# Attention and capped experts on one core: own first turn, quartered score tile, reordered closing steps

## The chip, the cores and the metric

The kernel runs on one core of a Trainium2 chip. TensorE (PE) multiplies, VectorE (DVE), ScalarE (ACT) and GpSimd (POOL) work on SBUF and PSUM, and SyncE (SP) and GpSimd issue most of the transfers. The metric is the device time of one execution in microseconds (us).

## The reference

Block-causal attention over 8 batches and 8 heads (576 positions, head size 64, blocks of 64), then a layer of 8 experts (512 to 1024 and back), each of which takes at most `capacity` (80) of the 4608 tokens.

```python
scores = where(block_i >= block_j, q @ k.T / sqrt(64), -1e9)
x      = softmax(scores) @ v                      # (4608, 512)
logits = x @ w_gate;  expert = argmax(logits);  gate = softmax(logits)[expert]
for e in range(8):                                # the 80 tokens with the largest gate
    out[tok] = gate[tok] * (relu(x[tok] @ w1[e]) @ w2[e])   # all other rows are 0
```

## The kernel before

**Attention** runs in turns, one for each pair of heads (32 pairs, 4 to a batch). `Pair.load` brings q and k in 32-column pieces (8 transfers of 72 KB on SP's queue, five turns ahead); `prep` transposes a piece-wise tile on VectorE, and for q GpSimd scales it into `QT`, a tile with a block of zeros in it (two passes, L476). `scores` multiplies for the five query tiles: "78", "56", "34", "12" of 128 rows, and the small tile "08", which holds the first and the last block of 64 rows. Before, the small tile is made of two products of full 128-row width per head that add up, each half of whose weight is the block of zeros (L495), and then a mask product (L506) writes large negative numbers over a block of the 56 tile. `max` takes row maxima on VectorE, `merge` the joint maximum of the first and last blocks' rows, `soft` the exponentials on ScalarE, which also sum the rows. `back` transposes the probabilities on TensorE block by block (L554) in groups B, A, C, L; `take` copies them out of PSUM on ScalarE or VectorE (L585); `values` multiplies with v (L574); `flip` turns the result on VectorE (L328), and `store` sends a batch to DRAM (`xs`) on SP's queue.

The order of each engine's work in this part is written out by hand: the list `TURN` (L38) is walked once per turn, and each entry names a pair relative to the turn's index and a step, so that a turn holds the scores and exponentials of the next pair and the transposes and values of its own. The turns before index 0 walk the same list with the pairs that exist; turn -1 thus runs the scores, maxima and exponentials of pair 0 in `TURN`'s order, with all the exponentials after `merge`. `LAST` is the list of the last turn. An engine takes its instructions in that order and waits at each for what it needs.

**Gating** is a side work of small steps: when a batch has been flipped, `enqueue` puts its steps on lists, and entries "pe", "t" and "ta" of `TURN` take one each: `recip`, `logits`, `products`, `shift`, `expo`, `first_of`, `weight`, `turn`, `turn2`, `placed`. They end in the table `Wt`. The last batch's steps are written out behind the loop (L685 to L715): row sums, the copies of the last values, logits, both last flips, `store`, `logits_out` (one half by ScalarE, one by VectorE), and so on to `placed`.

**Constants** are made in turn -2 (`constants`, `constants2`) ahead of the transposes of pair 0. The output rows are cleared by 18 transfers of 512 KB of zeros in the last five turns, on GpSimd's queue (L665).

**Selection** (L751 to L853): each partition's best values, ranks by products with triangular matrices, counts by compare-and-sum on VectorE and ScalarE, one-hot matrices, and products that pick token numbers into `gi`. From here on the order within an engine is the scheduler's, but for `issue_after`, which puts one instruction behind another. `warm` issues products whose result nobody reads: WARM[0] at the start, and WARM[1] to WARM[4] behind `turn2` of the last batch but one, `turn2` of the last, the ranks and the picks.

**Experts**: GpSimd gathers 80 rows for each expert (`xg`, L849), VectorE divides them by the row sums (`divide`, L937), TensorE transposes them (L963), multiplies with w1 (L954) and w2 (L1004), and GpSimd scatters the results (L1013). Weights come in 2 MB loads on SP's queue; three are there early, the fourth is issued behind the last batch's last store (L738), two more when the first gather has landed, the others after the fourth gather or as buffers come free.

## Time and profile before

| | us |
|---|---|
| runs | 420.0, 422.56, 422.8 (median 422.56) |
| profiled execution | 421.09 |
| its span | 419.3 |
| TensorE busy in it | 384.6 (92%) |
| ScalarE busy | 300.4 (72%) |
| VectorE busy | 279.6 (67%) |
| GpSimd busy | 141.7 (34%) |

Busy times are sums over the whole span. The turns run from about 16 to 286 us, gating and selection to about 315, the experts to the end. The end of a matmul is modelled, so TensorE's busy time holds waits as well. A line such as L554 is the line of the code that issued the instruction.

### The profile page before, as it was taken

What the parts mean: (1) busy time and instruction counts of PE and PEld (TensorE: products, weight loads), DVE (VectorE), ACT (ScalarE), POOL (GpSimd) and SP (SyncE); (2) the same over time, 40 slices, a digit from 0 to 9 for tenths busy, and PEclk for the clock granted to TensorE, in tenths of its full rate; (3) what the DMA queues carried; (4) which work ended last, traced back from release to release, by engine and by line L of the source; (5) the groups of instructions that cost most, each with busy time, mean ns of one, the idle gap of its engine ahead of it and who ended that gap; (6) DMA issues with size and microseconds to landing.
All of it is one profiled execution on the core that took longest, in us unless ns stands there. A gap on an engine that the chain in (4) does not pass through costs nothing. (4 is left out here: it accounts for less than half of the span.)

```text
span 419.3 us, 13895 instructions
## 1 busy us (share of the span) xinstructions
PE 384.6 (92%) x5359; PEld 256.4 (61%) x5359; DVE 279.6 (67%) x773; ACT 300.4 (72%) x950; POOL 141.7 (34%) x273
## 2 busy tenths in 40 slices
PE   5699999999999999999999999998877899999960
PEld 3566676666766676666676667666557745657420
DVE  5688888998899899899799989988743210100010
ACT  0699999999999999999999999996022132333340
POOL 6035332544336334354434545630246000000010
PEclk9699999999999999999999999999869899999995
DMA  9989999999999979999989899994649999998000
GB/s 122 146 124 181 148 195 142 220 174 144 193 188 173 147 157 169 139 201 173 150 177 155 151 132 327 373 353 114 172 176 292 383 398 388 395 399 316 20 19 19
DMA packets 199287, 84.31 MB, mean 201 GB/s; under 512 B 163677, under 2 KB 182109, under 8 KB 199216
## 3 DMA queue, kind: packets, MB, share of 16 engines
q1 hardware_dynamic: 187728, 56.35, 65.2%
q0 software_dynamic: 9120, 26.72, 21.7%
q8 instruction: 44, 0.72, 0.8%
q10 hardware_dynamic: 2368, 0.30, 0.6%
q14 instruction: 27, 0.22, 0.2%
HBM read 63.21 MB, written 20.33 MB: 199 GB/s over the span
## 5 line engine op out<-in xcount | busy, mean ns | idle before, releaser
L527 ACT ACTIVATE P<-bank,negm 128x192 f32<-128x192 f32 (+2 forms) x320 | 162.2, 591 | 0.0
L499 PE MATMUL bank<-T,qt 64*128 64x320 f32 (+3 forms) x512 | 107.1, 507 | 5.7 <-ACT P L527 3.9
L516 DVE TENSOR_REDUCE negm<-bank 128x1 f32<-128x192 f32 (+1 forms) x192 | 87.8, 472 | 25.9 <-PE bank L506 25.7
L585 ACT COPY PT<-bank 128x512 f32<-128x512 f32 (+1 forms) x190 | 90.3, 586 | 8.0 <-PE bank L554 8.0
L574 PE MATMUL bank<-PT,vn 128*64 128x384 f32 (+5 forms) x768 | 93.8, 384 | 0.9 <-ACT PT L585 0.9
L527 ACT ACTIVATION_READ_ACCUMULATOR P<-bank,negm 128x1 f32 x320 | 89.6, 281 | 0.0
L554 PEld LDWEIGHTS bank<-ident,P 64*128 64x128 f32 x1664 | 65.6, 140 | 19.4 <-ACT PT L585 19.2
L477 POOL TENSOR_SCALAR qt<-T 128x512 f32<-128x512 f32 x64 | 28.0, 449 | 145.8 <-DVE raw L516 131.8
L574 PEld LDWEIGHTS bank<-PT,vn 128*64 128x64 f32 x768 | 47.6, 137 | 40.8 <-issue 31.2
L554 PE MATMUL bank<-ident,P 64*128 64x64 f32 x1664 | 72.2, 226 | 0.0
L499 PEld LDWEIGHTS bank<-T,qt 64*128 64x128 f32 x512 | 43.6, 187 | 20.4 <-issue 7.4
L470 DVE STREAM_TRANSPOSE T<-ld 128x576 f32<-128x576 f32 x64 | 49.1, 768 | 0.2
L516 DVE TENSOR_REDUCE raw<-bank 128x1 f32<-128x64 f32 (+1 forms) x128 | 48.6, 435 | 0.6 <-PE bank L499 0.6
L463 POOL DMA_DIRECT2D vn<-in_v_dram x58 | 45.8, 792 | 1.0 <-PE bank L506 0.7
L954 PE MATMUL ps<-xsT,w 128*64 128x80 f32 x1024 | 40.2, 238 | 2.4 <-issue 1.9
L954 PEld LDWEIGHTS ps<-xsT,w 128*64 128x64 f32 x1024 | 38.0, 141 | 5.9 <-issue 4.6
L1008 DVE SCALAR_TENSOR_TENSOR y<-av,comb,yt 80x512 f32<-80x512 f32 x7 | 5.2, 746 | 50.2 <-ACT yt L1007 50.2
L1004 PE MATMUL av<-w,hT 128*32 128x512 f32 (+1 forms) x280 | 37.5, 594 | 0.0
L1013 POOL DMA_INDIRECT out_dram<-y,si x8 | 7.4, 925 | 78.2 <-DVE y L1008 78.2
L1007 ACT ACTIVATE yt<-ps,gfar 32x512 f32<-32x512 f32 (+1 forms) x18 | 11.4, 635 | 28.5 <-PE ps L1004 28.4
L496 PEld LDWEIGHTS bank<-T,qt 64*128 64x128 f32 x256 | 23.7, 191 | 11.6 <-issue 10.8
L1004 PE MATMUL ps<-w,hT 128*32 128x512 f32 (+1 forms) x72 | 29.1, 547 | 0.0
(175 smaller groups left out, 395.2 us busy)
## 6 DMA issues: line engine op xcount, KB each, us to landing
w<-in_moe_w_dram SPq DMA_DIRECT2D x13, 2048.0 KB, 19.8
ld<-in_q_dram SPq DMA_DIRECT2D x128, 72.0 KB, 4.2
xs<-Y SPq DMA_DIRECT2D x32, 288.0 KB, 5.7
out_dram<-zero POOLq DMA_DIRECT2D x18, 512.0 KB, 7.1
ld<-in_k_dram SPq DMA_DIRECT2D x124, 72.0 KB, 4.2
vn<-in_v_dram POOLq DMA_DIRECT2D x58, 128.0 KB, 4.3
w<-in_moe_w_dram POOLq DMA_DIRECT2D x8, 512.0 KB, 5.9
w<-in_moe_w_dram POOLq DMA_DIRECT2D x8, 256.0 KB, 5.9
```

Of the source, the lines that this page charges most:

```text
L463: eng.dma_start(self.vn[:, h], v[b, h0 + h, 0:512].rearrange("(j p) d -> p j d", p=P))
L470: nc.vector.transpose(t, self.nat[x].rearrange("p g d -> p (g d)"))
L477: nc.gpsimd.tensor_scalar(to, from_, scalar1=SCALE, scalar2=1.0, op0=ALU.mult, op1=ALU.mult)
L496: nc.tensor.matmul(s[h][:, c:c + n], lhsT=q_[:, b0:b0 + P], rhs=k_[:, k0:k0 + n], start=False, stop=False)
L499: nc.tensor.matmul(s[h][:, c:c + n], lhsT=q_[:, BLK + P * t:BLK + P * (t + 1)], rhs=k_[:, 0:n], start=(c == 0), stop=(g == "1"))
L516: nc.vector.tensor_reduce(to[:, b, h:h + 1], self.s[g][h][:, c:c + n], axis=AX.X, op=ALU.max, negate=True)
L527: nc.scalar.activation(Pt[self.i % 2][u][:, h, 0:n], self.s[g][h][:, c:c + n], AF.Exp, bias=self.negm[:, t, h:h + 1], scale=1.0, accum_out ...
L554: nc.tensor.transpose(pt[c][:, n_ * BLK:(n_ + 1) * BLK], row[u][r, h, P * j:P * (j + 1)], ident[r, r])
L574: nc.tensor.matmul(to, lhsT=self.vt[:, h, :] if j == 4 else self.vn[:, h, j, :], rhs=self.PT[:, h, row, b0:b1].rearrange("p b r -> p (b r) ...
L585: (nc.scalar.copy if (eng or TAKE[x]) == "a" else nc.vector.tensor_copy)(*self.out.pop(x))
L954: yield nc.tensor.matmul(dst(b)[64 * c:64 * (c + 1)], lhsT=w_[:, a, col:col + 64], rhs=x_[:, a], start=(a == 0), stop=(a == n - 1))
L1004: last = nc.tensor.matmul(to[col:col + s1 - s0, c0:c1], lhsT=hT[:, a, s0:s1], rhs=w_[:, a, c0:c1], start=(a == ends[0]), stop=(a == ends[1 ...
```

## The change

- The warming products become 8, 5, 5, 2 and 10.
- Turn -1 walks a list of its own, `FIRST`: pair 1's q is prepared ahead of pair 0's scores, each exponential of the 56 tile follows its maximum, the small tile's exponentials come right after `merge`, and so on.
- One exponential of a column of ones (`early_exp`) is issued on ScalarE in turn -4. The constants are made in turn -4, what needs their sums in turn -1, and the rest in turn 1.
- The small tile: one product per head and half, of a 64-column weight, into its own half of the rows, with no block of zeros; `QT` has 576 columns and GpSimd scales them in one pass; the mask of the 56 tile, 64 rows wide, comes ahead of the small tile.
- The clears of the last five turns go to SP's queue.
- Behind the loop: the steps left of the last batch but one come first; the reciprocals come after the values' copies; ScalarE copies both halves of the logits; only the flip of the last pair but one stays ahead of them. The steps of `first_of` and `weight` are interleaved, and the flip of the last pair and the store come after `turn`.
- In the selection the ranks' products keep their written order, the first slot step stands behind the counts, and the one-hot matrices are made in four pieces. `divide` works in four pieces, one per pair of heads, not two.

```diff
-WARM = [8, 10, 5, 2, 12]
+WARM = [8, 5, 5, 2, 10]
...
+FIRST = (
+    (LEAD, "load"),
+    (1, "begin"),
+    (2, "prep", 0),
+    (1, "scores", "2"),
+    (1, "max", "56", 0),
+    (1, "soft", "56", 0),
+    (1, "max", "56", 1),
+    (1, "soft", "56", 1),
+    (1, "scores", "1"),
+    (1, "scores", "3"),
+    (1, "max", "78", 0),
+    (1, "max", "78", 1),
+    (1, "max", "08", 0),
+    (1, "max", "08", 1),
+    (1, "merge"),
+    (2, "prep", 1),
+    (1, "soft", "08", 0),
+    (1, "soft", "08", 1),
+    (1, "soft", "78", 0),
+    (1, "soft", "78", 1),
+    (1, "max", "12", 0),
+    (1, "max", "34", 0),
+    (1, "max", "12", 1),
+    (1, "max", "34", 1),
+    (1, "soft", "12", 0),
+    (1, "soft", "34", 0),
+    (1, "soft", "12", 1),
+    (3, "load_v"),
+)
+
...
-                copy = nc.vector.tensor_copy if c and self.b == B - 1 else nc.scalar.copy
-                copy(lgT[:, BLK + 288 * c:BLK + 288 * (c + 1)], lt[c][:, 0:288])
+                nc.scalar.copy(lgT[:, BLK + 288 * c:BLK + 288 * (c + 1)], lt[c][:, 0:288])
...
                 self.T[1] = t
                 return
             self.T[0] = q_ = QT[self.i % 2]
-            ends, t_ends = [x_.rearrange("p (b c) -> p b c", c=BLK) for x_ in (q_[:, 0:3 * BLK], t)]
-            for to, from_ in ((q_[:, 3 * BLK:], t[:, BLK:]), (ends[:, 0:3:2], t_ends[:, 0:9:8])):
-                nc.gpsimd.tensor_scalar(to, from_, scalar1=SCALE, scalar2=1.0, op0=ALU.mult, op1=ALU.mult)
+            nc.gpsimd.tensor_scalar(q_, t, scalar1=SCALE, scalar2=1.0, op0=ALU.mult, op1=ALU.mult)

         def begin(self):
             self.negm = sm.tile([P, NT, 2], F32, name="negm", bufs=3)
...
         def scores(self, g):

             self.s[g] = s = banks("s" + g)
-            for u, c in GROUPS[g]:
+            rows = [slice(h * D, h * D + D) for h in range(2)]
+            for at, (u, c) in enumerate(GROUPS[g]):
                 t, n = TILES[u]
-                for h in range(2):
-                    r = slice(h * D, h * D + D)
+                last = u == GROUPS[g][-1][0]
+                if g == "2" and last:
+                    self.mask(g, BLK, False)
+                for h, r in enumerate(rows):
                     q_, k_ = self.T[0][r], self.T[1][r]
                     if u == "08":
-                        for b0, k0 in ((0, 0), (BLK, 512)):
-                            nc.tensor.matmul(s[h][:, c:c + n], lhsT=q_[:, b0:b0 + P], rhs=k_[:, k0:k0 + n], start=False,
-                                             stop=False)
+                        for half, b0 in ((0, 0), (BLK, 512)):
+                            nc.tensor.matmul(s[h][half:half + BLK, c:c + n], lhsT=q_[:, b0:b0 + BLK],
+                                             rhs=k_[:, b0:b0 + n], start=False, stop=True)
                     else:
-                        nc.tensor.matmul(s[h][:, c:c + n], lhsT=q_[:, BLK + P * t:BLK + P * (t + 1)], rhs=k_[:, 0:n], start=(c == 0),
-                                         stop=(g == "1"))
-            if g in MASKED:
-                ends = MASKED[g]
-                for h in range(2):
-                    r = slice(h * D, h * D + D)
-                    blocks = s[h].rearrange("p (u c) -> p u c", c=BLK)
-                    nc.tensor.matmul(blocks[:, ends[0]:ends[-1] + 1:max(ends[-1] - ends[0], 1)], lhsT=mrow[r],
-                                     rhs=mneg[r, 0:len(ends)], start=False, stop=True)
+                        nc.tensor.matmul(s[h][:, c:c + n], lhsT=q_[:, P * t - BLK:P * t + BLK], rhs=k_[:, 0:n],
+                                         start=(c == 0), stop=(g == "1"))
+            if g == "3":
+                self.mask(g, P, True)
+
+        def mask(self, g, m, stop):
+
+            ends = MASKED[g]
+            for h in range(2):
+                r = slice(h * D, h * D + D)
+                blocks = self.s[g][h][0:m].rearrange("p (u c) -> p u c", c=BLK)
+                nc.tensor.matmul(blocks[:, ends[0]:ends[-1] + 1:max(ends[-1] - ends[0], 1)], lhsT=mrow[r, 0:m],
+                                 rhs=mneg[r, 0:len(ends)], start=False, stop=stop)

         def group(self, u):
             return [(g, c) for g, us in GROUPS.items() for u_, c in us if u_ == u][0]
...

             for _ in range(4 if i >= n - 5 else 0):
-                clear(cleared)
+                clear(cleared, nc.sync)
                 cleared += 1
-            if i == -2:
+            if i == 1 - LEAD:
+                nc.scalar.activation(early_exp, ramp[:, 2, 0:1], AF.Exp)
                 constants()
+            if i == -1:
                 constants2()
             if i == 1:
                 constants3()
             if i >= 2 and i % 3:
                 next(early, None)
-            for d, what, *args in TURN if i < n - 1 else LAST:
+            for d, what, *args in FIRST if i == -1 else TURN if i < n - 1 else LAST:
                 if what in slots_:
                     slots_[what]()
                 elif 0 <= i + d < n and not (what == "flip" and n - NP <= i + d < n - 2):
...
                 enqueue(batches[(i - flipped) // NP])
         for _ in early:
             pass
+        while not turns:
+            t()
         bt = batches[B - 1]
-        for _ in bt.recip():
-            pass
         to, from_ = pairs[n - 1].out.pop("V0")
         half = to.shape[1] // 2
         pairs[n - 1].take("V1", "v")
         nc.scalar.copy(to[:, 0:half], from_[:, 0:half])
         nc.vector.tensor_copy(to[:, half:], from_[:, half:])
         lt = bt.logits_of()
-        for p_ in pairs[n - 2:]:
-            p_.flip()
-        bt.store()
+        for _ in bt.recip():
+            pass
+        pairs[n - 2].flip()
         bt.logits_out(lt)
-        ta()
-        while not turns:
-            t()
         bt.logits2()
         bt_, mark = turns.pop(0)
         bt_.turn2(banks("av")[0])
...
         bt.expo()
         while small:
             t()
-        for _ in (*bt.first_of(), *bt.weight()):
-            pass
+        found, weighed = bt.first_of(), bt.weight()
+        for g_ in (found, found, found, weighed, found, weighed, weighed):
+            next(g_)
         bt.turn(nc.vector, 2)
+        pairs[n - 1].flip()
+        bt.store()
         bt.turn2(banks("L")[0])
         for _ in bt.placed():
             pass
...
-    vec.scalar_tensor_tensor(slot[:, NH:], cnt_a, 0.5, pen[:, 1], op0=ALU.mult, op1=ALU.add)
+    with tc.issue_after(counted.ins):
+        vec.scalar_tensor_tensor(slot[:, NH:], cnt_a, 0.5, pen[:, 1], op0=ALU.mult, op1=ALU.add)
     vec.tensor_tensor(slot[:, 0:NH], cnt_v, pen[:, 0], op=ALU.add)
-    with tc.issue_after(one_hot(NH, NCAND).ins):
-        one_hot(0, NH)
+    hot = None
+    for c0 in (NH, NH + 3, 0, 3):
+        with ExitStack() as order:
+            if hot is not None:
+                order.enter_context(tc.issue_after(hot.ins))
+            hot = one_hot(c0, c0 + 3)
     for i in (*range(NH, NCAND), *range(NH)):
         picked = nc.tensor.matmul(pick[0:CHUNK, 0:3 * E], lhsT=OH[:, i], rhs=RI[:, i].rearrange("p k e -> p (k e)"),
                                   start=(i == NH), stop=(i == NH - 1))
...

-        v = src[:, 0:DM].rearrange("s (h i r c) -> s h r i c", h=2, i=2, r=NP)
-        r_ = src[:, DM:DM + H].rearrange("s (r h) -> s h r", h=2)
-        d = dst.rearrange("s (r h i c) -> s h r i c", r=NP, h=2, i=2)
-        for h in range(2):
-            last = vec.tensor_tensor(d[:, h], v[:, h], r_[:, h].unsqueeze(2).unsqueeze(3).broadcast_to([CHUNK, NP, 2, 32]),
-                              op=ALU.mult)
+        v = src[:, 0:DM].rearrange("s (h i r c) -> s r h i c", h=2, i=2, r=NP)
+        r_ = src[:, DM:DM + H].rearrange("s (r h) -> s r h", h=2)
+        d = dst.rearrange("s (r h i c) -> s r h i c", r=NP, h=2, i=2)
+        for r in range(NP):
+            last = vec.tensor_tensor(d[:, r], v[:, r], r_[:, r].unsqueeze(2).unsqueeze(3).broadcast_to([CHUNK, 2, 2, 32]),
+                                     op=ALU.mult)
         return last


```

## Rows read from the trace of the kernel before

**Rows 1.** Waits, 27 to 286 us, ScalarE and weight loads: total us, times, longest.

```profile
ACT PT L585 <- PE bank L554: 6.0, 13, 0.6
...
PEld bank L554 <- ACT PT L585: 18.6, 30, 0.6
```

**Rows 2.** Timeline of the opening: start, us, work, count, idle before and its releaser.

```profile
10.32 1.16 DVE L516 TENSOR_REDUCE negm<-bank 128x1 f32<-128x448 f32 x2 [1.68 <-PE bank L506]
...
12.08 1.51 DVE L516 TENSOR_REDUCE raw<-bank 128x1 f32<-128x64 f32 x4
...
12.35 1.28 ACT L527 ACT_TABLE_LOAD   x1 [12.35 <-DVE raw L516]
...
13.63 0.22 DVE L520 SCALAR_TENSOR_TENSOR negm<-raw,lower 128x4 f32<-128x4 f32 x1
13.64 0.63 ACT L527 ACTIVATE P<-bank,negm 128x448 f32<-128x448 f32 x1
...
16.05 2.03 PE L499 MATMUL bank<-T,qt 64*128 64x448 f32 x3 [3.89 <-ACT P L527]
...
20.57 0.58 ACT L585 COPY PT<-bank 128x512 f32<-128x512 f32 x1 [1.83 <-PE bank L554]
...
23.48 0.68 ACT L527 ACTIVATE P<-bank,negm 128x448 f32<-128x448 f32 x1
```

**Rows 3.** Stretches on TensorE: us, busy (count), granted clock, DMA share, GB/s.

```profile
14.00:16.00 2.00, 0.00 (x0) 0.54 1.01 160
...
20.00:21.00 1.00, 1.00 (x24) 0.51 0.86 186
```

**Rows 4.** Timeline of one turn on TensorE, from values to the block transposes.

```profile
155.19 0.28 PE L574 MATMUL bank<-PT,vt 128*64 128x64 f32 x4
...
155.30 0.29 PE L574 MATMUL bank<-PT,vn 128*64 128x64 f32 x4
...
155.52 1.02 PE L499 MATMUL bank<-T,qt 64*128 64x448 f32 x4
...
156.38 0.66 PE L496 MATMUL bank<-T,qt 64*128 64x64 f32 x8
...
156.80 0.25 PE L554 MATMUL bank<-ident,P 64*128 64x64 f32 x1
```

**Rows 5.** Timeline of the end of attention, VectorE.

```profile
293.14 1.43 DVE L328 STREAM_TRANSPOSE Y<-xT 128x576 f32<-128x576 f32 x2
...
294.50 0.42 DVE L353 COPY lgT<-bank 128x288 f32<-128x288 f32 x1
```

**Rows 6.** Timeline from gating to the first divide.

```profile
296.78 4.07 PE L595 MATMUL ps<-identr 128*128 128x512 f32 x10
...
298.99 0.56 DVE L406 TENSOR_TENSOR sp<-Gm,sameE 128x160 f32<-128x160 f32 x2
...
300.77 0.37 PE L415 MATMUL bank<-sp,sameR 128*32 128x40 f32 x16
...
310.24 1.12 POOL L849 DMA_INDIRECT xg<-xs,gi  x1 [4.61 <-DMA w<-in_moe_w_dram]
...
313.38 0.76 DVE L943 TENSOR_TENSOR xn<-xg 80x256 f32<-80x256 f32 x2 [4.04 <-DMA xg<-xs,gi]
```

**Rows 7.** Timeline of SP's queue at the last stores.

```profile
296.76 1.63 SPq L335 DMA_DIRECT2D xs<-Y  x1
298.78 1.27 SPq L288 DMA_DIRECT2D w<-in_moe_w_dram  x1
```

**Rows 8.** DMA issues, one each: KB, us to landing (issued at 312.96, 314.23, 296.76, 298.78).

```profile
xg<-xs,gi POOLq DMA_INDIRECT x1, 4.2
...
xg<-xs,gi POOLq DMA_INDIRECT x1, 8.7
...
xs<-Y SPq DMA_DIRECT2D x1, 288.0 KB, 5.6
...
w<-in_moe_w_dram SPq DMA_DIRECT2D x1, 2048.0 KB, 11.3
```

More of the change, by code (lines that the diff above doesn't have):

```diff
@@ L227, in tile_attn_moe @@
     dl = sm1.tile([P, NT, E + 1], F32, name="dl")
+    early_exp = sm1.tile([P, 1], F32, name="early_exp")
     def constants():
@@ L237, in constants @@
         nc.gpsimd.memset(lgT[:, 0:BLK], 0.0)
-    def constants2():
-        nc.vector.tensor_reduce(sameE, ident.rearrange("p (e j) -> p e j", j=16), axis=AX.X, op=ALU.add)
         nc.gpsimd.memset(sameR3, 0.0)
-        nc.vector.tensor_reduce(sameR, ident.rearrange("p (e j) -> p j e", j=16), axis=AX.X, op=ALU.add)
-        nc.gpsimd.tensor_copy(same.rearrange("p (e j) -> p e j", j=16), sameE.unsqueeze(2).broadcast_to([P, E, 16]))
         nc.gpsimd.memset(ones, 1.0)
@@ L248, in constants2, with constants3 @@
         nc.gpsimd.iota(iota_p, pattern=[[0, 1]], base=0, channel_multiplier=1, allow_small_or_imprecise_dtypes=True)
-        nc.gpsimd.affine_select(out=before, in_=same, compare_op=ALU.is_gt, fill=0.0, base=0,
-                                pattern=[[1, P]], channel_multiplier=-1)
-        nc.gpsimd.affine_select(out=after, in_=same, compare_op=ALU.is_gt, fill=0.0, base=0,
-                                pattern=[[-1, P]], channel_multiplier=1)
-        nc.gpsimd.tensor_tensor(before1, before, ident, op=ALU.add)
-        nc.gpsimd.tensor_tensor(after1, after, ident, op=ALU.add)
         nc.gpsimd.iota(iota_c, pattern=[[1, 16]], base=0, channel_multiplier=0,
                        allow_small_or_imprecise_dtypes=True)
+    def constants2():
+        vec, pool = nc.vector, nc.gpsimd
+        vec.tensor_reduce(sameE, ident.rearrange("p (e j) -> p e j", j=16), axis=AX.X, op=ALU.add)
+        vec.tensor_reduce(sameR, ident.rearrange("p (e j) -> p j e", j=16), axis=AX.X, op=ALU.add)
+        pool.tensor_copy(same.rearrange("p (e j) -> p e j", j=16), sameE.unsqueeze(2).broadcast_to([P, E, 16]))
+        pool.affine_select(out=before, in_=same, compare_op=ALU.is_gt, fill=0.0, base=0,
+                           pattern=[[1, P]], channel_multiplier=-1)
+        pool.affine_select(out=after, in_=same, compare_op=ALU.is_gt, fill=0.0, base=0,
+                           pattern=[[-1, P]], channel_multiplier=1)
+        pool.tensor_tensor(before1, before, ident, op=ALU.add)
+        pool.tensor_tensor(after1, after, ident, op=ALU.add)
+    def constants3():
         nc.vector.tensor_tensor(iota_c16, sameR, iota_c, op=ALU.mult)
         nc.vector.tensor_reduce(iota_r, iota_c16, axis=AX.X, op=ALU.add)
-    def constants3():
         nc.gpsimd.tensor_copy(cf, ci)
@@ L295, in tile_attn_moe @@
     Pt = [{u: pb.tile([P, 2, w], F32, name=f"P{u}_{i}") for u, w in WIDE.items()} for i in range(2)]
-    QT = [pb.tile([P, S + 2 * BLK], F32, name=f"qt{i}") for i in range(2)]
+    QT = [pb.tile([P, S], F32, name=f"qt{i}") for i in range(2)]
     VT = [pb.tile([P, 2, D], F32, name=f"vt{i}") for i in range(4)]
@@ L604, in tile_attn_moe @@
                 nc.gpsimd.memset(ps_[u][:, :, TILES[u][1]:w], 0.0)
-    for t_ in QT:
-        nc.gpsimd.memset(t_[:, BLK:2 * BLK], 0.0)
     for t_ in VT:
@@ L767, in tile_attn_moe @@
     HC = 16 * NH
+    ranked = None
     for h in (1, 0):
         pl = pall[h]
-        for k in range(2):
-            for g in range(2):
-                m = (before, after)[k] if g == h or k == h else (before1, after1)[k]
+        for k, g in ((k, g) for k in range(2) for g in range(2)):
+            m = (before, after)[k] if g == h or k == h else (before1, after1)[k]
+            with ExitStack() as order:
+                if ranked is not None:
+                    order.enter_context(tc.issue_after(ranked.ins))
                 ranked = nc.tensor.matmul(pl[:, g * HC:(g + 1) * HC], lhsT=m,
@@ L828, in one_hot @@
                                  iota_s.unsqueeze(1).broadcast_to([P, c1 - c0, CHUNK]), op=ALU.is_equal)
-    vec.scalar_tensor_tensor(slot[:, NH:], cnt_a, 0.5, pen[:, 1], op0=ALU.mult, op1=ALU.add)
+    with tc.issue_after(counted.ins):
+        vec.scalar_tensor_tensor(slot[:, NH:], cnt_a, 0.5, pen[:, 1], op0=ALU.mult, op1=ALU.add)
     vec.tensor_tensor(slot[:, 0:NH], cnt_v, pen[:, 0], op=ALU.add)
-    with tc.issue_after(one_hot(NH, NCAND).ins):
-        one_hot(0, NH)
+    hot = None
+    for c0 in (NH, NH + 3, 0, 3):
+        with ExitStack() as order:
+            if hot is not None:
+                order.enter_context(tc.issue_after(hot.ins))
+            hot = one_hot(c0, c0 + 3)
     for i in (*range(NH, NCAND), *range(NH)):
```

2 lines of the change are left out of this document (1 added, 1 removed).

## The prediction

> **What bounds the kernel now.** I read the waits by engine over the turns first. From 27 to 286 us ScalarE waited 6.0 us in all, in 13 of the 31 turns, each time for the block transposes of the pair in hand (L554); TensorE's weight loads waited 18.6 us for ScalarE's copies, in 30 turns [rows 1]. So ScalarE's stream sets the pace of the turns, and TensorE touches it only in those 13. What brings that stream forward at its start brings the end forward; what shortens TensorE's turn gains 6.0 us at the most.
>
> Second, the timeline of the opening [rows 2]. The first maxima start at 10.32, after an idle 1.68 of VectorE. The first exponential stands behind the merge and behind a table load of 1.28, and starts at 13.64. TensorE, idle for 3.89, begins pair 1 at 16.05. ScalarE's first copy waits 1.83 more and starts at 20.57, and pair 1's first exponential at 23.48. By the granted clock TensorE ran at 1.2 instead of 2.4 GHz from about 14.1 to 21.0 [rows 3].
>
> Third, one turn on TensorE [rows 4], and last the closing chain from the last logits to the first expert: the two flips, the logits' second copy behind them [rows 5], the spread weights, ten warming matmuls in front of the turning matmuls, the gather, the first divide [rows 6].
>
> **First turn.** Put ahead of the first maximum are one transposition (a flip of the same size is 1.43/2 = 0.71 [rows 5]) and two reductions, which I bound by the 0.58 of a 448-column maximum: 1.87 against a cover of 1.68 [rows 2], and these reductions used to stand ahead of the first transposes, which now start sooner. I take 10.32 as it is; without that cover it would be 1.9 later. The table load moves into the 12.35 that ScalarE idles before it [rows 2]: free. The first exponential then starts at about 10.95, not 13.64. The merge ends at 10.32 + 1.16 + 1.51 + 0.22 = 13.2. Two small exponentials follow (six took 16.05 - 13.64 = 2.41, 0.40 each), so pair 1's scores start at 14.0, **2.05 earlier**. That copy came 4.52 after pair 1's first scores, mostly at half clock: at worst 18.5 now. At full clock it would be 2.3 after, but the five exponentials left end at 17.2 at the latest, so 17.2. The gain at the copy is 2.1 to 3.4. The clock fell in a pause of 3.89 that becomes 1.8, so it may stay, or not: I take **-2.8**. The lower end is -1.0: TensorE spent 16.05 to 21.0 at half clock; if the whole stretch from 14.1 falls on turn 0, 2 us more at half speed give back 1.0. The upper end is -3.4. Past it the loads are ahead, and VectorE is waited for by nobody in [rows 1].
>
> **The quarters, 32 times.** From the small tile's first matmul to the first block transpose it is 156.80 - 156.38 = 0.42 [rows 4], eight matmuls in two row tiles, 0.1 per step. A step of 64 columns with a 64-column weight took 155.30 - 155.19 = 0.11 for two; the same four matmuls followed by another tile shape took 155.52 - 155.30 = 0.22. A change of shape therefore shows as 0.11. The new order has two more (64*128 to 64*64 and back), a mask step (0.06), two steps if all four quarters run at once (0.11), and some 0.05 of weight load no longer hidden: 0.44. If the halves of a head follow each other it is 0.60 with rounding up; if the change of shape is free 0.28. The mark on a turn is -0.14 to +0.18; I take +0.05, as the 0.11 is measured on this engine in this loop. It counts in the 13 turns where ScalarE waits: **+0.65**. Ends: 13 x -0.14 = -1.8, and 31 x 0.18 = +5.6 if the slack of the other turns is used up.
> The Trainium skill (TensorEngine Tiling (Array Packing), Key Properties) says that changing the tiling mode, not just the tile, drains the engine; it gives no time. The 0.11 agrees. Its Theoretical Speedup table says up to 2x for a dimension of 64 or less; by that alone the small tile would save half of its 0.42, about -2.7 over 13 turns, without the drains.
> The single scaling pass over 576 columns in place of two costs nothing: GpSimd is waited for by nobody in [rows 1].
>
> **Clears on SyncE.** 18 issues leave GpSimd's queue and join SP's behind the last loads of q and k; nothing but the stores of batch 6 stands behind them, which no engine needs for two turns. The bytes are the same. Nothing; without that cover the stores would land some microseconds later, still ahead of the gather.
>
> **The closing chain.** The logits' second copy goes from VectorE at 294.50, behind two flips, to ScalarE behind its first copy: 0.4 sooner. The interleaved seven small steps save about 0.2 of waits on one another. Five warming matmuls instead of ten (4.07 for ten [rows 6]) end before the spread weights are ready, so the turning matmuls start at 298.99 + 0.56 and not at 300.77: 1.2 sooner. The last flip, now behind the spread weights, holds the copy into the table for 0.3. Sum at that copy: -0.4 - 0.2 - 1.2 + 0.3 = -1.5. One-hot in quarters and the ranks head by head: -0.2, the gather issued at 308.5 instead of 310.24.
> But the stores of the last batch wait for the last flip. They began when both flips were done, 293.14 + 1.43 = 294.57, and will at 299.55 - 0.6 + 0.71 = 299.7, **5.1 later**. Behind them on SP's queue stands the next weight load: 298.78 [rows 7] goes to 303.9, and its landing 11.3 later [rows 8] to 315.2. The last store, issued at 296.76 and 5.6 in flight, lands at 307.5, just ahead of the gather. So the gather, which had the DMA engines to itself (313.38 - 310.24 = 3.14), now runs beside 2 MB of weights. With loads beside it a fetch took 4.2 (one that met them late) to 8.7 [rows 8]: landing at 311.6 (3.1) to 317.2. I take 4.5, near the row that met them late, since this load is halfway through by then: 313.0, -0.35. The divide in four pieces lets the transposes start on the first: -0.3. Sum **-0.65**; ends: 311.6 - 313.38 - 0.3 = -2.1, and 317.2 - 313.38 - 0.3 = +3.5. Two microseconds more come on top if the missing warming leaves the ranking at half clock; that would fall in the store's shadow.
>
> **Sum.** -2.8 + 0.65 - 0.65 = -2.8. The profiled execution took 421.09 (span 419.3), so 418.3. The runs are 420.0, 422.56 and 422.8, median 1.5 above the profiled one; I forecast **418.5**.
>
> **Rivals.**
> *The gather is not held up.* For it: only one load is in flight, and 3.14 is the clean time. Then the tail gives -2.1 and the sum is -4.25: 416.8. Chance 0.24.
> *The clock takes the opening back.* TensorE still pauses, and the fall at 14.1 came 2 us after its last matmul [rows 3]; all of turn 0 then runs at half clock: -1.0 + 0.65 - 0.65, 420.1. This is also the case in which the reordering hardly does what it says. Chance 0.20.
> *The quarters cost the loop*, the one that ends slower. Place: between the scores of the 448-column tile and the transposes ScalarE's copies wait for. Price: two drains (0.22), the halves in sequence (0.22), the mask (0.06), two weight loads unhidden (0.2): 0.70 against 0.42, +0.28 a turn; 3.6 in the 13 turns, 8.7 if all 31 come to wait. It decides from 0.11 a turn on, where 31 turns eat the 3.45 of the other two terms. At 8.7 the time is 421.09 - 3.45 + 8.7 = 426.3, at 3.6 it is 421.2; I price it at 424. Against it: TensorE waits for ScalarE in 30 turns [rows 1], so it has slack. The drain above is what the skill's rule would charge. Chance 0.13.
> *The forecast*, 417.5 to 420, has 0.38; 0.05 is left for a gather at 8.7 (422).
>
> **How the numbers follow.** About 1% (4.2 us) is what a measurement of this kernel can tell from no change: faster means under 418.3. All of the first rival and a third of the forecast's case lie there: 0.37. Slower (over 426.8) is part of the quarters' case: 0.08. The rest, 0.55, is within 1%. The range goes from 414.2, where the good ends of opening and tail (-3.4 - 2.1) and most of the quarters' (-1.4 of -1.8) meet, to 424.0, which takes in the gather's bad end and the quarters' case up to its price. The likeliest case alone is 417.5 to 420.
>
> **What would show it.** ScalarE's first exponential near 11 and pair 1's first near 20.6; the small tile's matmuls as 64*64 and the distance to the first transpose near 0.44; ScalarE's waits for L554 near 6 us; the turning matmuls close behind the spread weights; stores from 299.7 less the opening's gain, and the first fetch over 4 us from issue to landing. I am wrong if pair 1's first exponential moves by under 1.5, if ScalarE comes to wait for L554 in nearly every turn, or if the first fetch lands in about 3.

## The result, and the profile after

The changed kernel takes **417.4 us** (median of 6 runs, 416.4 to 417.9) against 421.8 for the kernel before beside it: ratio 0.9892, 95% interval 0.9868 to 0.9916, 4.6 us or 1.1% faster. The forecast was 418.5 in a range of 414.2 to 424.0. The time was inside the range, and in part by luck: of the four terms only the opening came as forecast. The quarters' cost did not come, the clears gained where nothing was expected, and the closing chain alone lost time where a gain was forecast, and these misses nearly cancel.

The opening, in the timeline of the changed kernel (start, us, work, count, idle before and its releaser), to be held against [rows 2]:

```profile
2.95 1.28 ACT L703 ACT_TABLE_LOAD   x1 [2.95 <-issue]
...
9.72 1.16 DVE L553 TENSOR_REDUCE negm<-bank 128x1 f32<-128x448 f32 x2
...
10.38 0.63 ACT L564 ACTIVATE P<-bank,negm 128x448 f32<-128x448 f32 x1 [5.94 <-DVE negm L553]
...
12.37 0.22 DVE L557 SCALAR_TENSOR_TENSOR negm<-raw,lower 128x4 f32<-128x4 f32 x1
...
13.47 1.25 PE L532 MATMUL bank<-T,qt 64*128 64x448 f32 x4 [1.82 <-ACT P L564]
...
17.70 0.58 ACT L622 COPY PT<-bank 128x512 f32<-128x512 f32 x1 [0.73 <-PE bank L591]
...
21.06 0.64 ACT L564 ACTIVATE P<-bank,negm 128x448 f32<-128x448 f32 x1
...
24.77 1.02 PE L532 MATMUL bank<-T,qt 64*128 64x448 f32 x4
```

The table load stands at 2.95, the first exponential at 10.38 and not behind the merge, pair 1's scores 2.58 earlier, pair 1's first exponential at 21.06 and not 23.48, the second turn's scores at 24.77 and not 26.90. The clock fell all the same; stretches on TensorE (us, busy (count), granted clock, DMA share, GB/s), against [rows 3]:

```profile
14.00:16.00 2.00, 2.00 (x30) 0.58 0.94 157
...
20.00:21.00 1.00, 1.00 (x9) 0.50 0.89 169
21.00:22.00 1.00, 1.00 (x12) 0.92 0.85 203
```

One turn on TensorE, against [rows 4], and ScalarE's waits from 24 to 283 us (total, times, longest), against [rows 1]:

```profile
152.65 1.02 PE L532 MATMUL bank<-T,qt 64*128 64x448 f32 x4
...
153.60 0.22 PE L543 MATMUL bank<-mneg,mrow 64*64 64x64 bf16 x2
...
153.61 0.35 PE L529 MATMUL bank<-T,qt 64*64 64x64 f32 x8
...
153.89 1.77 PE L591 MATMUL bank<-ident,P 64*128 64x64 f32 x48
```

```profile
ACT PT L622 <- PE bank L591: 5.0, 14, 0.5
```

From the small tile's first matmul to the first transpose it is now 153.89 - 153.61 = 0.28, where it was 0.42; from the second listed turn to the last (28 turns) the kernel needs 274.15 - 32.88 = 241.27 us, where it needed 277.66 - 35.10 = 242.56: 1.29 less. ScalarE's waits for the block transposes fell from 6.0 to 5.0 us.

The closing chain (timeline, all engines, then SyncE's queue), against [rows 5 to 7]:

```profile
289.99 0.91 ACT L385 COPY lgT<-bank 128x288 f32<-128x288 f32 x2 [0.81 <-PE bank L378]
...
295.17 0.52 PE L447 MATMUL bank<-sp,sameR 128*32 128x40 f32 x16 [2.06 <-DVE sp L438]
...
297.51 1.04 PE L813 MATMUL ps<-spread,before 128*128 128x96 f32 x4 [0.47 <-DVE spread L801]
...
300.05 1.06 PE L813 MATMUL av<-spread,after 128*128 128x96 f32 x4
...
306.26 1.14 POOL L893 DMA_INDIRECT xg<-xs,gi  x1 [5.92 <-ACT occ L940]
...
313.32 0.89 DVE L987 TENSOR_TENSOR xn<-xg 80x128 f32<-80x128 f32 x4 [7.94 <-DMA xg<-xs,gi]
```

```profile
296.07 3.82 SPq L368 DMA_DIRECT2D xs<-Y  x4
300.28 1.25 SPq L321 DMA_DIRECT2D w<-in_moe_w_dram  x1
```

The attention's last row of values products (called the last values product below) started 3.60 earlier than before (285.95, was 289.55), the gather 3.98 earlier (306.26, was 310.24 [rows 6]). Stores and weight load went out at 296.07 and 300.28. And the first divide, which waits for the first fetch, came at 313.32, where it was 313.38: **the whole lead of 4 us is gone**. The fetch, counted from the gather's start to the first divide, takes 7.06 us in place of 3.14 [rows 6]. The rankings ran at half clock, 1.04 to 1.06 a group of four products in place of 0.61 to 0.66.

The experts' part, timeline of TensorE in the changed kernel and then in the kernel before (L998 and L954 are the first layer, L1048 and L1004 the second):

```profile
315.20 1.34 PE L998 MATMUL ps<-xsT,w 128*64 128x80 f32 x16
...
323.06 4.23 PE L998 MATMUL ps<-xsT,w 128*64 128x80 f32 x116 [0.57 <-issue]
...
329.26 0.18 PE L948 MATMUL av<-chk,ones 128*128 128x10 bf16 x1 [1.41 <-issue]
...
332.85 0.62 PE L1048 MATMUL av<-w,hT 128*32 128x512 f32 x3
```

```profile
315.35 0.91 PE L954 MATMUL ps<-xsT,w 128*64 128x80 f32 x18 [0.51 <-ACT xsT L964]
...
322.87 0.91 PE L954 MATMUL ps<-xsT,w 128*64 128x80 f32 x19 [1.89 <-issue]
...
330.16 0.44 PE L881 MATMUL ps<-RG,OH 128*80 128x24 bf16 x7 [2.06 <-issue]
...
336.15 0.62 PE L1004 MATMUL av<-w,hT 128*32 128x512 f32 x3
```

Both begin at 315.2 to 315.4, but on 'issue', where TensorE waits for nothing that the profile shows, the changed kernel stands still for 0.57 + 1.41 us and the one before for 1.89 + 2.06. Its last scatter starts at 405.07, 2.24 earlier (407.31), and its span ends 10.5 after that, where it was 12.0: another 1.5 that no engine's computing explains. So the 3.7 us of span (419.26 to 415.54) add up as -2.13 (to the second turn's scores), -1.47 (to the last values product), -0.38 (to the gather), **+3.92** (the fetch), -2.18 (to the last scatter), -1.48 (behind it).

### The profile page after: what moved, and what is told of

It is laid out like the page before. It is cut to its first block, busy times and chain, and to the rows that moved or that the text cites. A ratio compares the mean times of both kernels' runs of the same rounds, so it can differ in the third digit from the quotient of the medians.

```text
span 415.5 us, 13862 instructions
## 1 busy us (share of the span) xinstructions
PE 381.5 (92%) x5352; PEld 241.7 (58%) x5352; DVE 281.9 (68%) x790; ACT 300.8 (72%) x952; POOL 126.1 (30%) x221
## 3 DMA queue, kind: packets, MB, share of 16 engines
q0 software_dynamic: 6528, 17.28, 16.0%
## 5 line engine op out<-in xcount | busy, mean ns | idle before, releaser
L564 ACT ACTIVATION_READ_ACCUMULATOR P<-bank,negm 128x1 f32 x320 | 90.4, 285 | 0.0
L591 PEld LDWEIGHTS bank<-ident,P 64*128 64x128 f32 x1664 | 63.7, 141 | 22.7 <-ACT PT L622 19.0
L591 PE MATMUL bank<-ident,P 64*128 64x64 f32 x1664 | 71.3, 228 | 0.2 <-ACT P L564 0.2
L507 POOL TENSOR_SCALAR qt<-T 128x576 f32<-128x576 f32 x32 | 21.2, 662 | 148.8 <-DVE raw L553 146.2
L532 PEld LDWEIGHTS bank<-T,qt 64*128 64x128 f32 x512 | 44.2, 189 | 17.8 <-issue 5.8
L998 PE MATMUL ps<-xsT,w 128*64 128x80 f32 x1024 | 39.5, 238 | 0.6 <-issue 0.6
L998 PEld LDWEIGHTS ps<-xsT,w 128*64 128x64 f32 x1024 | 37.5, 140 | 4.0 <-ACT yt L1051 1.7
L1048 PE MATMUL av<-w,hT 128*32 128x512 f32 (+1 forms) x280 | 37.5, 594 | 0.0
L1048 PE MATMUL ps<-w,hT 128*32 128x512 f32 (+1 forms) x72 | 29.1, 548 | 0.0
L1018 ACT ACTIVATE hT<-ps 128x320 f32<-128x320 f32 x16 | 7.0, 438 | 26.7 <-PE ps L998 26.6
```

The costliest lines, as they stand in the source:

```text
L507: nc.gpsimd.tensor_scalar(q_, t, scalar1=SCALE, scalar2=1.0, op0=ALU.mult, op1=ALU.mult)
L532: nc.tensor.matmul(s[h][:, c:c + n], lhsT=q_[:, P * t - BLK:P * t + BLK], rhs=k_[:, 0:n], start=(c == 0), stop=(g == "1"))
L564: nc.scalar.activation(Pt[self.i % 2][u][:, h, 0:n], self.s[g][h][:, c:c + n], AF.Exp, bias=self.negm[:, t, h:h + 1], scale=1.0, accum_out ...
L591: nc.tensor.transpose(pt[c][:, n_ * BLK:(n_ + 1) * BLK], row[u][r, h, P * j:P * (j + 1)], ident[r, r])
L998: yield nc.tensor.matmul(dst(b)[64 * c:64 * (c + 1)], lhsT=w_[:, a, col:col + 64], rhs=x_[:, a], start=(a == 0), stop=(a == n - 1))
L1048: last = nc.tensor.matmul(to[col:col + s1 - s0, c0:c1], lhsT=hT[:, a, s0:s1], rhs=w_[:, a, c0:c1], start=(a == ends[0]), stop=(a == ends[1 ...
```

## The experiments

All are timed against the kernel before on the same chip; a ratio of 0.0024 is one microsecond.

**The opening alone** (before, with the new order of the first turn, the early exponential, the constants).
```diff
-            for d, what, *args in TURN if i < n - 1 else LAST:
+            for d, what, *args in FIRST if i == -1 else TURN if i < n - 1 else LAST:
```

> The kernel before with the first turn's own order, the early exponential and the moved constants alone. Theory (the opening's gain lasts): the second turn's scores start some 2.1 us earlier than before (26.90), as in the changed kernel (24.77), and the run is 1.9 to 2.5 us faster than before. Rival (the half clock of the opening, 14 to 21 us, takes it back, or the loop absorbs it): the second turn's scores start early, but the run is within 0.7 us of before. The forecast's own term was 2.8 us.

Measured: 0.9924 (0.9898 to 0.9950), **3.2 us faster**. The second turn's scores started at

```profile
23.53 1.02 PE L532 MATMUL bank<-T,qt 64*128 64x448 f32 x4
```

In the profiles of all fourteen kernels that score step came at 24.6 us on the mean in the nine with the new order (23.06 to 25.26) and at 27.3 in the five without it (26.63 to 28.45): 2.7 earlier, against 2.8 forecast. The time gained is a little more than this theory's 1.9 to 2.5, with an interval of 2.1 to 4.3; the rival, that clock or loop takes it back, falls.

**The quarters alone.**
```diff
-    QT = [pb.tile([P, S + 2 * BLK], F32, name=f"qt{i}") for i in range(2)]
+    QT = [pb.tile([P, S], F32, name=f"qt{i}") for i in range(2)]
...
+                            nc.tensor.matmul(s[h][half:half + BLK, c:c + n], lhsT=q_[:, b0:b0 + BLK],
+                                             rhs=k_[:, b0:b0 + n], start=False, stop=True)
```

> The kernel before with the small score tile in quarters alone (its mask ahead of it, its queries taken from the one scaled tile). Theory from the changed kernel's trace (the quarters are a gain: between the second turn's scores and the last values product it needs 261.18 us against 262.65): 1.0 to 1.8 us faster than before, about 0.05 us in each turn, the small tile's first quarter 0.28 us ahead of the first transpose where its first half was 0.42 us. Rival (the forecast's term): 0.65 us slower, the loop's gain then coming from the opening. Second rival: no change within 0.5 us.

Measured: 0.9994 (0.9969 to 1.0018), no difference that shows. In its trace the same 28 turns take 276.07 - 34.82 = 241.25, the 1.3 less of the changed kernel; but the profiled execution, one of the two slowest of eleven (424.99), then loses 5.1 in the last turn, from its first scores to the last values product (timeline of that turn):

```profile
278.51 0.78 DVE L328 STREAM_TRANSPOSE Y<-xT 128x576 f32<-128x576 f32 x1 [3.81 <-DMA xs<-Y]
...
280.16 0.95 PE L559 MATMUL bank<-ident,P 64*128 64x64 f32 x16 [1.63 <-DVE xT L590]
```

VectorE's turning waits 3.81 us for a store of the array that it writes, and TensorE 1.63 for VectorE. So the loop's gain is in all nine traces with the quarters (241.3 to 241.5, against 242.6 to 242.8 in the five without), the forecast's cost of 0.65 in none. As a time it is not resolved: the interval, 1.3 us faster to 0.8 slower, holds both.

**The closing chain alone** (before, with the turnings and stores late, fewer warming products, the new order of rankings and one-hot).
```diff
-        for p_ in pairs[n - 2:]:
-            p_.flip()
-        bt.store()
+        pairs[n - 2].flip()
         bt.logits_out(lt)
...
         bt.turn(nc.vector, 2)
+        pairs[n - 1].flip()
+        bt.store()
```

> The kernel before with the closing chain's edits alone (order of turnings and stores, fewer warming products, both logits copies on ScalarE, the rankings' and one-hot's order). Theory (the first fetch waits for the weight load that now runs beside it, and the experts' first products get most of that back because their later fetches were issued earlier): first fetch 6 to 7.5 us from issue to use against 3.1, first expert product 3 to 4 us later than before, and yet the run within 1 us of before (-0.7 to +0.5). Rival A (the late fetch is simply paid): 2.5 to 4 us slower than before. Rival B (the forecast: 0.65 us faster, first fetch in 4.5 us).

Measured: 1.0039 (1.0019 to 1.0059), **1.6 us slower**, between the theory and rival A. Timeline:

```profile
309.32 1.12 POOL L855 DMA_INDIRECT xg<-xs,gi  x1 [5.04 <-issue]
...
317.27 0.76 DVE L949 TENSOR_TENSOR xn<-xg 80x256 f32<-80x256 f32 x2 [9.65 <-DMA xg<-xs,gi]
...
319.82 6.37 PE L960 MATMUL ps<-xsT,w 128*64 128x80 f32 x144
```

The fetch takes 7.95 us, the first expert product comes 4.47 later than before, and 2.2 of these are back at the last scatter (409.57 - 407.31 = 2.26 later).

**The weight load behind the fetch** (changed kernel).
```diff
-    with tc.issue_after(bt.stored.ins):
-        weights(1)
...
-    weights(FWA - 1, fetches[0])
+    weights(FWA, fetches[0])
```

> The changed kernel with its fourth weight load issued behind the first fetch, not ahead of it. Theory (that load holds the fetch): the first fetch lands 3 to 4 us after its issue at about 306.3 and no longer 7.1, the first expert product starts 3 to 4 us earlier than the changed kernel's 315.20, and the run is 2.5 to 3.9 us faster than the changed kernel (413.5 to 415, ratio 0.980 to 0.985 to before). Rival A (the last Y stores hold it, not the weight load): the fetch stays at 6 to 7 us and the time within 0.7 us of the changed kernel. Rival B (the lead is spent again in the experts' opening, on later fetches and stalls of TensorE's queue): the first expert product early, the time within 1 us of the changed kernel.

Measured: 1.0089 (1.0057 to 1.0121), 8.4 us slower than the changed kernel, which neither the theory nor a rival had. The fetch took 3.12, and the first expert product came at 310.98, 4.2 earlier, as expected; TensorE's timeline at the end shows the loss, first layers of two experts in a row (245 products) and then waits of 2.77 and 3.06:

```profile
376.14 8.72 PE L996 MATMUL ps<-xsT,w 128*64 128x80 f32 x245
...
389.59 0.64 PE L1046 MATMUL pm<-w,hT 128*32 128x256 f32 x3 [2.77 <-SPq L1084]
...
409.40 0.41 PE L1046 MATMUL pm<-w,hT 128*32 128x256 f32 x3 [3.06 <-DVE y L1050]
```

The experts' products are ordered by the compiler's planner, and with this edit it chose another order: in the compiled order the last expert's second layer, whose weights land last, stood ahead of those of two earlier experts. The short fetch rules out rival A, as the stores went out as late as in the changed kernel (from 296.23). What the earlier fetch is worth this time cannot say. So I wrote the order out (first layers of 0, 1 and 2, second layers of 0 and 1, then in turn) and repeated it.

**The written order, alone, with the load behind the fetch, and on the kernel before.**
```diff
+        if chain[0] is not None:
+            order.enter_context(tc.issue_after(chain[0].ins))
+        chain[0] = make()
```

> The changed kernel with the order of the experts' products written out (first layers of experts 0, 1 and 2, second layers of 0 and 1, and then first and second in turn) where a planner chose it. Theory: the planner's order in the changed kernel was already close to this one, so the time stays within 1 us of 417.4. Rival: the planner's order costs something of its own, and the time falls by 1.5 us or more.

> The same written order with the fourth weight load behind the first fetch. Theory (the load holds the fetch, and the 8 us lost in the run with the load moved were the planner's other order at the end, where the last expert's second layer stood ahead of two earlier ones): first expert product at 311 as there, no stall over 2 us after 385, and 2.4 to 3.9 us faster than the same order with the load ahead (413.5 to 415). Rival (the weights are the bound: the stream that starts 5 us later ends later, whatever the order): 4 us or more slower than the changed kernel again.

> The kernel before with the same written order of the experts' products. Theory (order by itself is neutral, and the 20.8 us from the first expert product to the first second-layer product were late fetches and the half clock): within 1 us of before. Rival (the planner's order of the kernel before was the worse one, and the change gained by getting another): 2 us or more faster than before, and then the gain of the change shrinks to under 3 us between the two kernels in this order.

Measured: changed kernel in this order 0.9908 (0.9889 to 0.9926), 417.98; with the load behind the fetch **0.9857 (0.9835 to 0.9879), 416.64**; kernel before in it 1.0024 (1.0010 to 1.0038), 422.99. The order by itself changes little: 0.7 us slower by the ratios on the changed kernel, inside the intervals, and 1.0 slower (0.4 to 1.6) on the kernel before. The change gains 1.0024 - 0.9908, 4.9 us, in it: a lucky plan is not what made the changed kernel faster. Moving one load then brings 0.0051, 2.2 us (1.3 by the medians), a little under the 2.4 to 3.9 expected. Timeline:

```profile
305.23 1.14 POOL L891 DMA_INDIRECT xg<-xs,gi  x1 [4.56 <-issue]
...
308.43 0.90 DVE L985 TENSOR_TENSOR xn<-xg 80x128 f32<-80x128 f32 x4 [4.42 <-DMA xg<-xs,gi]
...
310.95 1.33 PE L1005 MATMUL ps<-xsT,w 128*64 128x80 f32 x16
```

The fetch takes 3.20, where with the load ahead of it, in the same order, it takes 8.08 (304.18 to 312.26). **The load holds the fetch.** Of the 4.20 us at the first expert product (315.15) 2.26 are left at the first second-layer product (332.94, was 335.20) and 0.65 at the last scatter (404.94, was 405.59). But the attention ended 1.08 later in this execution (286.27, was 285.19): counted from the last values product the lead is 5.28, then 3.34, then 1.73, which fits the time. In the run with the load ahead five scatters in a row follow each other by 9.87 us, here by up to 10.3, and TensorE once waits for a weight load (timeline of TensorE):

```profile
361.02 0.62 PE L1052 MATMUL av<-w,hT 128*32 128x512 f32 x3 [0.23 <-DMA w<-in_moe_w_dram]
```

**The stores early again** (changed kernel in the written order, both turnings and the store ahead of the logits).
```diff
-        pairs[n - 2].flip()
+        for p_ in pairs[n - 2:]:
+            p_.flip()
+        bt.store()
...
-        pairs[n - 1].flip()
-        bt.store()
```

> The written order, with both last turnings and the store back ahead of the logits copies, the rest of the closing chain as changed. Theory (the later store and load hold the first fetch): first fetch 3 to 4 us from issue to use, its issue 0 to 1.5 us later than in the changed kernel relative to the last values product (20.3 us there), and 2 to 4 us faster than the written order with the store late (413.5 to 415.5). Rival (the turning products and copies cost the gating chain what the fetch gains): the same within 1 us.

Measured: 0.9890 (0.9866 to 0.9913), 417.62. The fetch is back at 3.27 (306.28 to 309.55), with store and load both early; its start is 19.7 us behind the last values product, not later than in the changed kernel (20.3), but 0.7 later than in the written order with the store late (18.99). Against that order it is 0.4 us faster by the medians and 0.8 by the ratios, inside both intervals: the gain expected did not come.

**Without the closing edits** (written order, with the opening, quarters, clears and divide as changed; the closing block, rankings and one-hot as before).
```diff
-WARM = [8, 5, 5, 2, 10]
+WARM = [8, 10, 5, 2, 12]
...
-        for g_ in (found, found, found, weighed, found, weighed, weighed):
-            next(g_)
+        for _ in (*bt.first_of(), *bt.weight()):
+            pass
```

> The changed kernel with the written order of the experts' products and the closing chain (turnings, stores, warming, rankings, one-hot) as it was before. Theory (the closing edits lose by the held-up fetch what the chain gains, as in the run with them alone, 1.6 us slower than before): first fetch in 3 to 4 us, and 0.7 to 2.2 us faster than the written order with the closing edits (417.98). Rival (together with the earlier attention the closing edits are worth their 0.65 us): 0.5 to 1.5 us slower than that.

Measured: 0.9899 (0.9870 to 0.9927), 417.96, against 0.9908 with them: neither side shown. Fetch 3.09.

**The clears on SyncE alone.**
```diff
-                clear(cleared)
+                clear(cleared, nc.sync)
```

> The kernel before with the clears of the output issued by SyncE in place of GpSimd, and nothing else. Theory (GpSimd's last drain grows with the transfers that it issued: 4.98 us in every run whose clears it issued, 3.51 us in every run without them): the drain falls to 3.51 us, the last scatter to the end of the span takes 10.4 us in place of 12.0, and the run is 1.2 to 1.8 us faster than before. Rival (the forecast, nothing): within 0.5 us of before, because the drain is shorter only where something else in those kernels made it so, or because SyncE's clears delay the last loads by as much.

Measured: 0.9954 (0.9935 to 0.9972), **1.9 us faster**. The last scatter starts at 407.41 and the span ends at 417.7, 10.3 later. What became shorter is GpSimd's long DRAIN behind the last scatter, as the trace records it (start in us, ns):
```
before              413.436  4977 GpSimd DRAIN
after               410.901  3507 GpSimd DRAIN
the clears alone    413.354  3507 GpSimd DRAIN
```
It is 4977 in all five kernels whose clears GpSimd issues, and 3507 in all nine where SyncE does. The software queue carried 9120 packets before and 6528 after. These are the only two counts, so how the drain grows between them is not shown.

**More warming behind the picks** (with the stores early).
```diff
-WARM = [8, 5, 5, 2, 10]
+WARM = [8, 5, 5, 2, 18]
```

> The run with both turnings and the store early (417.62) with 18 warming products behind the picks in place of 10, so that TensorE works until the first fetched rows are there. Theory (the half clock from 310 to 316 is paid because TensorE sat idle from 307.6 to 309.9): the granted clock stays 1.00 there, expert 0's first layer takes 5 to 6 us in place of 9, and the run is 1.5 to 3 us faster, 414.6 to 416.1. Rival (what comes next in TensorE's queue is late anyway: its instructions under full DMA engines, or the weights): the clock stays up, the stalls on 'issue' grow by as much, and the time is within 0.7 us of 417.6.

Measured: 0.9931 (0.9909 to 0.9954), 1.7 us slower than 10 of them. The granted clock was 1.00 from 310 to 318, and TensorE stood still instead:

```profile
313.08 1.69 PE L1007 MATMUL ps<-xsT,w 128*64 128x80 f32 x40
315.85 0.30 PE L1007 MATMUL ps<-xsT,w 128*64 128x80 f32 x2 [1.08 <-issue]
316.60 0.23 PE L1007 MATMUL ps<-xsT,w 128*64 128x80 f32 x1 [0.44 <-issue]
317.32 0.36 PE L1007 MATMUL ps<-xsT,w 128*64 128x80 f32 x3 [0.50 <-issue]
...
318.74 5.18 PE L1007 MATMUL ps<-xsT,w 128*64 128x80 f32 x95 [0.48 <-issue]
```

One to three products at a time, 0.7 us apart. As in the rival, TensorE was late anyway: expert 0's first layer took 10.3 us (313.08 to 323.42), where with 10 warming products, at half clock to 316.7, it took 8.5 (311.99 to 320.46). How much slower the warming made the run is not shown, since its rankings ran at half clock besides (1.01 to 1.06 a group) and its gather went out 1.4 us later behind the last values product (21.1, not 19.7).

**All loads behind the last fetch.**
```diff
-    HOLD = 3
+    HOLD = E - 1
...
-    weights(FWA, fetches[0])
+    weights(FWA, fetches[-1])
```

> The run with the fourth weight load behind the first fetch and the written order (416.64), with all weight loads from the fourth on held behind the eighth fetch (issued at 314.3 there). Theory (while the loads fill the DMA engines, TensorE's instructions arrive late: its stalls on 'issue' in expert 0's first layer end when a 16 KB transfer of the instruction queue lands): all fetches land 3 to 4 us after their issue, expert 0's first layer has no stall over 0.3 us and ends by 317 to 319, the first second-layer product starts 2 to 6 us earlier than 332.9, and, as each load still comes ahead of its use (from 317 on, one in 5.1 us), the run is 1.5 to 5 us faster, 411.6 to 415.1. Rival A (the loads bound the stage, 10.1 us for an expert against 9.87 of TensorE): the first layers come early, but the end moves by less than 1 us or gets later. Rival B (the stalls have nothing to do with the loads): they stay as they are, and the time is the same or later.

Measured: 0.9918 (0.9895 to 0.9941), 418.54: 1.9 us slower by the medians than with the loads behind the first fetch, 2.6 by the ratios. TensorE's timeline:

```profile
316.66 3.00 PE L1005 MATMUL ps<-xsT,w 128*64 128x80 f32 x79 [0.90 <-issue]
...
327.09 2.71 PE L1005 MATMUL ps<-xsT,w 128*64 128x80 f32 x72 [0.98 <-DMA w<-in_moe_w_dram]
...
333.77 0.63 PE L1005 MATMUL ps<-xsT,w 128*64 128x80 f32 x11 [2.13 <-issue]
```

The fetches land in 3.0 to 3.3, so the loads are out of the way. But the stall after some 50 products, 1.00 us with the loads behind the first fetch, is still 0.90 with no load under way, and expert 0's first layer takes 8.5 us in both. The theory falls. TensorE then waits 0.98 for a weight load at 327, as rival A has it, and 2.13 on 'issue' ahead of 333.77, where it was 1.71, as rival B has it: both have a part, and the run does not divide it.

## Why the prediction was right, and where it was not

**The first turn: right.** -2.8 was forecast; the step measures 2.7 earlier and the time 3.2 (2.1 to 4.3). Each landmark came within 0.6 us: first exponential 10.95, is 10.38; merge 13.2, is 12.37 + 0.22 = 12.6; pair 1's scores 14.0, are 13.47; first copy 17.2 to 18.5, is 17.70; pair 1's first exponential 20.6, is 21.06. The rival of the clock had its mechanism right, turn 0 runs at 1.2 GHz in the changed kernel from about 14.3 to 21, and its price too high. In two kernels (the opening alone and the written order) the clock did not fall there, and the second turn's scores came at 23.53 and 23.06; but their next turn took 8.9 us where it takes 8.1 to 8.2 in the others, and the third turn's scores, at 32.39 and 31.91, were 1.0 on the mean ahead of the other seven with the new order. In four of those the half clock lay on the first turn's scores instead (four products in 1.87, not 1.02), and it cost as much. So it costs some 1.0, not the whole gain.

**The quarters: the wrong sign in the traces.** The step that failed is "A change of shape therefore shows as 0.11", charged twice. The distance is 0.28, the value that the forecast gave for a change that is free. The 0.11 is still there in the place that it was read from (the changed kernel, TensorE):

```profile
32.55 0.28 PE L611 MATMUL bank<-PT,vt 128*64 128x64 f32 x4
32.66 0.29 PE L611 MATMUL bank<-PT,vn 128*64 128x64 f32 x4
32.88 1.02 PE L532 MATMUL bank<-T,qt 64*128 64x448 f32 x4
```

The first four products take 0.11, the four ahead of the scores 0.22. So it belongs to that place and not to every change of shape. And by the forecast's own terms a turn would have cost 0.44 - 0.42 = 0.02, not the 0.05 that it took. The Trainium skill (TensorEngine Tiling (Array Packing), Key Properties) says that a change of the tiling mode drains the engine; no run here shows a cost of it. The gain came where the forecast counted it, in the turns in which ScalarE waits: its waits fell by 1.0 us (5.0 in 14 turns, were 6.0 in 13), most of the loop's 1.29. That is some 0.1 in each, where the forecast had 0.14 for a free change.

**The clears: a term that was missed.** "The bytes are the same. Nothing" looked for an engine that waits for the transfers. Nobody does, but the kernel ends with GpSimd's drain, and 1.47 us of it went with the 18 clears. The row to look at was the end of the span, 12.0 us behind the start of the last scatter.

**The closing chain: the held fetch foreseen but mis-sized, and the gain ahead of it not there.** Stores "from 299.7 less the opening's gain" came at 296.07 (299.7 - 3.6 = 296.1), the load at 300.28 (forecast 303.9 - 3.6). The fetch beside it was taken as 4.5, "since this load is halfway through by then"; it is 7.06 to 8.08 in the three kernels with that load still in flight and 3.1 to 3.4 in the others. It ends about when the load does: issued at 300.28 and 12.7 in flight, the load lands at 312.9, and the divide starts at 313.32; in the closing chain alone it lands at 317.8, and the divide starts at 317.27. The half clock in the rankings, which was to fall "in the store's shadow", did: in the written order the rankings had the full clock and the gather went out 1.3 sooner behind the last values product (18.99, not 20.31), but the first divide only 0.3 sooner (27.07, not 27.37).
The forecast also took 1.7 us off the gather's start by the shorter chain. Most of this was the clock's: the execution that it read had the half clock from 297.5 to 300.9, and its gather came 20.7 behind the last values product. With the old chain at full clock there (the opening alone, the kernel before in the written order, the clears alone) it came at 19.2; with the new chain at full clock at 18.95 to 18.99 in the three written-order runs with the store late, and at 19.4 in the closing chain alone. At the same clock the edits are worth 0.3 at most.

**What the sum left out** is behind the fetch. From the first expert product to the last scatter it takes 89.8 to 90.4 us in the three kernels where the fetch is held, and 92.0 to 96.3 in those with an early one (the planner's odd order left out), the kernel before among them (91.96). So some 2 us and more of a late start come back. TensorE needs 9.87 us for an expert, and with the load behind the fetch some scatters came 10.1 to 10.3 apart; that the loads are this second limit is read from one wait of 0.23 and not shown. Stalls on 'issue', in part at half clock, take more from the early starts. What ends those stalls is not settled, but the fourteen traces divide them. Fourteen stalls of 0.57 to 2.13 us, all those behind expert 0's first layer that are over 0.4, end 1.33 to 1.59 us after a transfer of 16,384 bytes on the instruction queue has ended. Those within expert 0's first layer show no such distance, and one of them, of 0.90, is there without loads. The Trainium skill (Runtime: NRT & Kernel Launch, Instruction fetch mechanics) has instructions refilled in blocks of 16 KiB, mostly hidden; if that is the cause, it is not hidden here, and no run shows it by itself.

Together: -3.2 (opening), -0.3 (quarters, as timed), -1.9 (clears), +1.6 (closing chain alone) make -3.8, and the whole measured -4.6 (3.5 to 5.6): within the intervals of the parts. Against the forecast's -2.8, +0.65, 0 and -0.65 the misses are -0.4, -0.9, -1.9 and +2.2. They add up to -1.0 because the closing chain's miss has the other sign; that the total came so near is luck, apart from the opening. The pieces of the divide were not tried alone.

## What to carry to other kernels

The end of a span is a row like any other: work issued through GpSimd's queue can come back as a longer drain after everything else is done. A small fetch that is on the critical path has to be issued, and the bulk loads held, so that none stands ahead of it; look at which queue holds what at that time, not only at how many bytes are in flight. A lead won ahead of a stage can be spent in it, here 5.28 us at its first product and 1.73 at its last scatter: look at what the stage waits for before pricing the lead. And a chain whose time is read from an execution at half clock must be compared at the same clock.

## What the runs showed of the hardware that I had not expected

GpSimd's long drain at the end took 4977 ns with 137 transfers issued by it and 3507 with 119, the same to the nanosecond in every kernel of a kind. With the clock at 2.4 GHz behind more warming, TensorE gained nothing: in expert 0's first layer it stood still for 1.08 + 0.44 + 0.50 + 0.36 + 0.48 us and took 10.3 (313.08 to about 323.4), where the same kernel with less warming, at 1.2 GHz to 316.7, took 8.5, and the changed kernel, at 1.2 GHz to about 318 and with no stall, 6.3 (315.20 to 321.5). Two more changes of tile shape in a turn cost no time that can be seen (0.28 us from the small tile to the transposes, where it was 0.42). And an edit to one load moved 8 us at the other end of the kernel through the planner's order: with the order written out it did not.
